# Reading the states' rows of two batches together, and dividing them by their softmax sums as they leave PSUM, in an attention and feed-forward kernel on one Trainium2 core

## The chip, the cores and the metric

The kernel runs on one core of one Trainium2 chip. The metric is the time of one execution in microseconds of the device. Most of the discussion uses one profiled execution, whose span runs from its first to its last instruction.

A core has five engines with a queue of instructions each: TensorE (PE; its weight loads are listed as PEld), VectorE (DVE), ScalarE (ACT), GpSimd (POOL) and SyncE (SP), which here only issues DMAs. Each works through its queue in order and waits for the others by semaphores. Products land in PSUM; all other operands lie in SBUF.

## The reference

Eight batches, eight heads, 512 tokens of 64 values, and 32 states of 64 values for each batch and head. Tokens read the states, states read the tokens, and all rows (544 for each batch) go through a two-layer feed-forward.

```python
scores = scale * np.matmul(x, state.transpose(0, 1, 3, 2))     # (8, 8, 512, 32)
scores = scores - scores.max(-1, keepdims=True)
a = np.exp(scores)
a /= a.sum(-1, keepdims=True) + 1e-09
xread = np.matmul(a, state)
scores2 = scale * np.matmul(state, x.transpose(0, 1, 3, 2))    # (8, 8, 32, 512)
scores2 = scores2 - scores2.max(-1, keepdims=True)
a2 = np.exp(scores2)
a2 /= a2.sum(-1, keepdims=True) + 1e-09
sread = np.matmul(a2, x)                                       # the states' rows
attn_out = np.concatenate([xread, sread], axis=2)
# rows of 8 heads x 64 values side by side: (4352, 512)
h = rows @ w_in                                                # 512 -> 2048
g = np.maximum(0.01 * h, h)
out = g @ w_out                                                # 2048 -> 512
```

The change concerns `a2` and `sread`.

## The kernel before

One batch at a time is in the main loop (line 932, batches 2 to 7; batches 0 and 1 are worked off by code written out ahead of it). A batch has 16 steps `s`. Step `s` makes one block of 128 hidden features for the batch's 512 tokens (`ff1`, line 369: two products into a PSUM tile with the tag "ph", and a leaky ReLU on ACT into `hT`). Between these, `fill(s)` inserts units of the second layer (line 557; of the batch before, then of this one), by the fixed table `PACE`. Also between the steps stands the attention of the next batch `nxt`: scores at s = 1, the tokens' softmax at s = 1 to 7, the states' softmax at s = 3 (maximum), 7 and 8 (`a_exp2`, ACT's exponential of 512 tokens with its sum beside it, in two halves `g`) and 11 (`a_probs2`). At s = 10 come the products of M (`a_m`, line 351, state times first-layer weights) for `nxt`: `pm0`, `pm1` and `pm2`, 8 products each; `pm2` has two tiles of the tag "ph" and is evicted by DVE and ACT (line 1031).

The order on every engine is the order of the program text. PSUM tags and their buffers set who waits for whom: the tag "ph" has two buffers of one bank, so each new "ph" tile waits for the eviction of the one before the last. The pool `att` has two buffers for each tag, unless stated.

The path of the states' rows:

- `a_exp2` (line 274) writes `e2`, 128 partitions (4 pairs of heads x 32 states) x 2 halves x 512 tokens, and its sums `r2`.
- `a_probs2` (line 279) adds 1e-9 to the sums, takes the reciprocal `qc`, and multiplies `e2` by it into `a2`, two instructions of 128x512 on DVE (line 285).
- `a_a2t` (line 290) issues a transposing DMA from SP, `a2` to `a2T`, at s = 0 of the batch's own loop (for batches 0 and 1 ahead of the loop).
- `a_sread_rows` (line 311) makes the rows on PE: 32 products of 128x64 for a batch, into a "ph" tile `psn` (line 318). ACT copies it to `sr_n` (line 326). It is called for batch 0 at s = 1 of batch 2, for batches 1 and 2 together at s = 10 of batch 2, and for batches 3, 4, 5 and 6 at s = 10 of their own loops, each time just ahead of `pm0`.
- `sread_t` (line 330) transposes `sr_n` into `sr_t` by DMA: batches 0 to 3 in batch 4, batches 4 to 6 in batch 7. Batch 7's own rows go another way (`a_sread`).

In the loop of batch 2, DVE also makes four sums of the second layer's weights (`weights_sum`, line 523): sums 0 and 2 at s = 3, sums 1 and 3 at s = 8. At s = 1, `a_sread_rows([a0])` is written ahead of `a_shift(nxt)` (lines 216 to 226, DVE). POOL casts the next loaded batch to bf16 (line 105) and the states (line 176).

Of the kernel before, what the change touches and what calls it, by code (L numbers as in the profile page):

```python
# [9 lines left out]
P = 128  # L10
B, H, S, D = 8, 8, 512, 64
# [8 lines left out]
BF16 = mybir.dt.bfloat16  # L20
FP32 = mybir.dt.float32
AF = mybir.ActivationFunctionType
ALU = mybir.AluOpType
# [4 lines left out]
def kernel(  # L28
# [9 lines left out]
    nc = tc.nc  # L38

    consts = ctx.enter_context(tc.tile_pool(name="consts", bufs=1))  # L40
    wpool = ctx.enter_context(tc.tile_pool(name="wpool", bufs=1))
    xpool = ctx.enter_context(tc.tile_pool(name="xpool", bufs=4))
    att = ctx.enter_context(tc.tile_pool(name="att", bufs=2))
# [53 lines left out]
    def load_x(b, eng):  # L97
        xl[b] = xpool.tile([P, H, NT * D], FP32, name="xl", tag="xl", bufs=1)
        eng.dma_start(xl[b][:], x[b].rearrange("h (p t) d -> p h (t d)", t=NT))

    def open_xb(b):
        xs[b] = xpool.tile([P, NT, H, D], BF16, name="xb", tag="xb")
# [37 lines left out]
    st_t = [consts.tile([P, hi - lo, P], BF16, name=f"st_t{lo}") for lo, hi in groups]  # L140
    sr_t = consts.tile([P, B, NK, NS], BF16, name="sr_t")
    sr_n = {}

    stb0 = consts.tile([P, 4, D], BF16, name="stb0")

# [132 lines left out]

    def a_probs2(a):
        nc.vector.tensor_scalar(out=a.r2[:], in0=a.r2[:], scalar1=1e-9, scalar2=None, op0=ALU.add)  # L280
        q2 = att.tile([P, 2], FP32, name="qc", tag="qc")
        nc.vector.reciprocal(q2[:], a.r2[:])
        a.a2 = att.tile([P, 2, S], BF16, name="a2", tag="a2")
        for g in range(2):
            nc.vector.tensor_scalar(
                out=a.a2[:, g, :], in0=a.e2[:, g, :],
                scalar1=q2[:, g:g + 1], scalar2=None, op0=ALU.mult,
            )

    def a_a2t(a):  # L290
        a.a2T = att.tile([P, 2, NT, P], BF16, name="a2T", tag="a2T")
        nc.sync.dma_start_transpose(
            a.a2T[:].rearrange("p g i q -> p (g i) q"), a.a2[:].rearrange("p g s -> p (g s)")
        )
# [16 lines left out]
    def a_sread_rows(some):  # L311

        ps = psum.tile([P, len(some), 2, D], FP32, name="psn", tag="ph")
        for u, a in enumerate(some):
            for g in range(2):
                for i in range(NT):
                    for k in range(NK):
                        nc.tensor.matmul(  # L318
                            ps[NS * k:NS * (k + 1), u, g, :],
                            lhsT=a.a2T[:, g, i, NS * k:NS * (k + 1)], rhs=a.xb[:, i, 2 * k + g, :],  # L320
                            start=(i == 0), stop=(i == NT - 1),
                        )
        c, b0 = divmod(some[0].b, 4)
        if c not in sr_n:
            sr_n[c] = consts.tile([P, 4, P], BF16, name=f"sr_n{c}", tag=("st0f", "stf2")[c])
        nc.scalar.copy(
            sr_n[c][:, b0:b0 + len(some)], ps[:].rearrange("p u g d -> p u (g d)")
        )

    def sread_t(c, n):  # L330
        nc.sync.dma_start_transpose(
            sr_t[:, 4 * c:4 * c + n].rearrange("p b k n -> p b (k n)"),
            sr_n[c][:, :n].rearrange("p b q -> p (b q)"),
        )

# [33 lines left out]
    def ff1(a, hT, j):  # L369
        ph = psum.tile([P, S], FP32, name="ph", tag="ph")  # L370
        for g in range(2):
            nc.tensor.matmul(  # L372
                ph[:], lhsT=a.M[:, g, P * j:P * (j + 1)],
                rhs=a.aT[:, g, :],
                start=(g == 0), stop=(g == 1),
            )
        nc.scalar.activation(out=hT[:, j, :], in_=ph[:], func=AF.Prelu, alpha=0.01)  # L377
# [265 lines left out]
    att_of = [Attn() for _ in range(B)]  # L643
    a0, a1, a2 = att_of[:3]
# [150 lines left out]
    def open_ff1_0(tag):  # L795
        if tag == "sc":
            pr = psum.tile([P, 2, S], FP32, name="php", tag=tag, bufs=1)
            return pr, [pr[:, 0], pr[:, 1]]
        ph = [psum.tile([P, S], FP32, name="ph", tag=tag) for _ in range(2)]
        return ph, [p[:] for p in ph]  # L800
# [15 lines left out]
    t0, b0 = open_ff1_0("py")  # L816
# [32 lines left out]
    for u in range(2):  # L849
        ps = psum.tile([P, NT, 2, P], BF16, name="pxt2", tag="ph")  # L850
# [81 lines left out]
    for b in range(2, B):  # L932
        hT = hpool.tile([P, 16, S], BF16, name="hT", tag="hT")
        a = att_of[b]
        nxt = att_of[b + 1] if b + 1 < B else None
        now = Batch(b, hT)
        std = []
        if b == 2:
            std = [(i, 3) for i in range(2)] + [(i, jq) for i in range(2, NT) for jq in range(4)]

        def fill(s):
            n = (PACE2 if b == 2 else PACE)[s]
            left = min(n, len(before.units)) if before else 0
            if left:
                before.run(left)
            if n > left:
                now.run(n - left)

        for s in range(16):
            if s == 11:  # L950
                fill(s)
            ff1(a, hT, s)
            if s == 0:
                if b + 2 < B:
                    load_x(b + 2, nc.sync)
                    open_xb(b + 2)
                a_a2t(a)
                if before:
                    for n in (0, 1):
                        before.f.sums(n, 4, 8)  # L960
            elif s == 1:
                if nxt is not None:
                    a_scores(nxt)
                m_evict(a, 3, a_m(a, 3, "big"), SCA)
                if b == 2:
                    a_sread_rows([a0])
                if nxt is not None:
                    a_shift(nxt)
                if b + 2 < B:
                    for h in range(0, H, 2):  # L970
                        cast_x(b + 2, h, h + 2, POO)
                if before:
                    before.f.sums(2, 4, 8)
            elif s == 3:
                if before:
                    before.f.sums(3)
                if nxt is not None:
                    a_max2(nxt)
                if b == 2:
                    weights_sum(0)  # L980
                    weights_sum(2)
            elif s == 4:
                if b == 2:
                    state_t(1)
                elif b == 4:
                    sread_t(0, 4)
                elif b == 7:
                    sread_t(1, 3)
            elif s == 8:
                if nxt is None:  # L990
                    a_sread(a)
                if b == 2:
                    weights_sum(1)
                    weights_sum(3)
            elif s == 12:
                for n in range(3):
                    now.f.sums(n, 0, 4)
            if nxt is None:
                if s == 4:
                    fi = FastIn(None)  # L1000
                    for n in range(3):
                        fi.w_sum(n)
                elif s == 10:
                    fi.w_sum(3)
                    fi.x_sums()
            if s == (9 if b == 2 else 7) and b + 2 < B:
                a_open(att_of[b + 2], b + 2)
                a_xt_dma(att_of[b + 2])
            if nxt is not None:
                if s == 5:  # L1010
                    a_exp(nxt)
                elif s in (7, 8):
                    a_exp2(nxt, s - 7)
                    if s == 7:
                        a_probs(nxt)
                elif s == 11:
                    a_probs2(nxt)
                elif s in (12, 13):
                    SCA(nxt.M[:, s - 12, DM:2 * DM], pm1[:, s - 12, :])
            if std:  # L1020
                i, jq = std.pop(0)
                piece(1, h1, i, jq)
            elif s != 11:
                fill(s)
            if s == 10 and nxt is not None:
                a_sread_rows([a1, a2] if b == 2 else [a])
                pm0 = a_m(nxt, 0, "big")
                pm1 = a_m(nxt, 1, "sc")
                pm2 = a_m(nxt, 2, "ph")
                for g, copy in enumerate((VEC, SCA)):  # L1030
                    copy(nxt.M[:, g, 2 * DM:3 * DM], pm2[g][:])
                m_evict(nxt, 0, pm0, SCA)
        before = now
# [24 lines left out]
    u, v = [psum.tile([P, 1, HC], FP32, name="yu", tag="ph")[:] for _ in range(2)]  # L1058
# [8 lines left out]
    for n in (1, 2, 6, 5, 7, 3, 4):  # L1067
# [7 lines left out]
        elif n == 7:  # L1075
            nc.gpsimd.tensor_tensor(
                out=ysb[1][:, :, HC:], in0=fs.sv[7][:], in1=fs.sv[5][:], op=ALU.add
# [8 lines left out]
    for i in range(2):  # L1086
        bank = before.bank[7] if i == 0 else psum.tile([P, 2, HC], FP32, name="yz", tag="big", bufs=1)[:]
        for m in range(NM):
            before.f.unit(bank, 4, m, first=True, of=i)
        nc.vector.tensor_tensor(  # L1090
            out=before.yo(1)[:, i, :HC], in0=bank[:, i, :], in1=before.f.sv[7][:, i, :], op=ALU.add
# [32 lines left out]
```

## Time and profile before

| | before |
|---|---|
| median of 3 runs | 204.49 us (204.19 to 204.7) |
| time of the profiled execution | 204.49 us |
| its span | 202.7 us |
| PE busy | 197.0 us, 97% |
| DVE busy | 151.4 us, 75% |
| ACT busy | 143.7 us, 71% |
| POOL busy | 39.7 us, 20% |
| 14 + 2 scalings of `e2` (line 285, DVE) | 4.9 us, 350 ns each |
| 6 copies of the rows (line 326, ACT) | 265 ns for 128x128 (five), 372 ns for 128x256 (one) |

The profile's page gives busy time by engine, the chain of work that ended last, and groups of instructions by line. The trace behind it can be asked for the order of instructions in a window (start, length, engine, line, output and inputs, count, and in brackets the idle time ahead and what ended it) and for who waited for whom. "ended last" matters most: an engine off that chain can be made faster without any effect.

### The profile page before, as it was taken

To read this page: it belongs to the slowest core of one execution; us is meant where nothing else is said; L and a number is where in the kernel's file an instruction comes from. 1 tells how busy PE (TensorE), PEld (TensorE's weight loads), DVE (VectorE), ACT (ScalarE), POOL (GpSimd) and SP (SyncE) were. 2 spreads that over 40 slices of the span, in tenths; PEclk is the share of its full clock that TensorE was granted. 3 is DMA by queue.
4 is the path that set the end of the run, shared out by engine and by line. 5 is a ranking of instruction groups with operands and counts; after the bars stand their busy time and mean duration, and the time that the engine had idled before them with its cause. 6 is when DMAs were issued, how large, how long until landed. Compare 5 with 4: busy or idle time off the path is not lost.

```text
span 202.7 us, 4755 instructions
## 1 busy us (share of the span) xinstructions
PE 197.0 (97%) x1964; PEld 126.0 (62%) x1964; DVE 151.4 (75%) x230; ACT 143.7 (71%) x265; POOL 39.7 (20%) x66
## 2 busy tenths in 40 slices
PE   7899999999999999999999999999999999999993
PEld 2543544444344567766776767766767677799882
DVE  1677679599799969976996699769968853686612
ACT  3458848589869796978697878788778856467710
POOL 8831002021005005200251040200020002004250
PEclk9999999999999999999999999999999999999999
DMA  6999996999477895537946795250017100410035
GB/s 189 223 207 277 229 298 113 141 303 245 53 175 214 114 275 109 103 125 253 118 29 181 240 127 105 103 159 5 0 57 198 27 0 32 178 55 0 3 89 170
DMA packets 39733, 27.99 MB, mean 138 GB/s; under 512 B 25312, under 2 KB 36704, under 8 KB 39712
## 3 DMA queue, kind: packets, MB, share of 16 engines
q1 hardware_dynamic: 34512, 20.88, 44.6%
q0 software_dynamic: 4912, 6.55, 15.8%
q10 hardware_dynamic: 288, 0.26, 0.6%
q8 instruction: 15, 0.25, 0.5%
q14 instruction: 6, 0.05, 0.1%
HBM read 17.30 MB, written 8.91 MB: 129 GB/s over the span
## 4 chain that ended last, share of the span: by engine, by line
PE 96%; DVE 1%; ACT 1%; issue 0%
PE yq L557 36%; PE ph L372 23%; PE py L487 10%; PE pm L351 4%; PE pyw L487 3%; PE pf L441 3%; PE yu L557 3%; PE pspin L132 3%; PE ph L804 2%; PE sc L206 1%; PE psn L318 1%; PE phw L383 1%; PE php L804 1%; DVE M L365 1%; ACT xT L666 1%; PE scn L695 0%
## 5 line engine op out<-in xcount | busy, mean ns | idle before, releaser
L377 ACT ACTIVATE hT<-ph 128x512 bf16<-128x512 f32 x108 | 63.5, 604 | 22.0 <-PE ph L372 21.4
L372 PE MATMUL ph<-aT,M 128*128 128x512 bf16 x216 | 62.3, 379 | 0.0
L557 PEld LDWEIGHTS <-su 128*128 128x128 bf16 x416 | 39.7, 98 | 14.5 <-DVE su L546 1.7
L557 PEld LDWEIGHTS <-hT 128*128 128x128 bf16 x288 | 27.7, 98 | 11.7 <-issue 1.1
L557 PE MATMUL yq<-tw_xf,su 128*128 128x256 bf16 x192 | 27.2, 273 | 0.0
L105 POOL CAST xb<-xl 128x512 bf16<-128x512 f32 (+1 forms) x21 | 14.4, 724 | 65.2 <-PE ph L372 40.6
L557 PE MATMUL yq<-w_out_bf,hT 128*128 128x256 bf16 x192 | 27.0, 273 | 0.0
L372 PEld LDWEIGHTS <-M 128*128 128x128 bf16 x216 | 21.0, 98 | 9.3 <-issue 0.8
L546 DVE TENSOR_TENSOR su<-hT 128x1024 bf16<-128x1024 bf16 x24 | 16.8, 700 | 10.5 <-ACT hT L377 10.5
L487 PE MATMUL py<-w_out_bf,hT 128*128 128x512 bf16 x96 | 24.2, 379 | 0.0
L487 PEld LDWEIGHTS <-hT 128*128 128x128 bf16 x128 | 12.1, 98 | 14.6 <-issue 0.9
L627 POOL TENSOR_TENSOR yo<-sv,sv 128x512 f32<-128x512 f32 x6 | 7.8, 1300 | 54.1 <-ACT sv L566 42.7
L569 DVE TENSOR_TENSOR yo<-yq,sv 128x512 f32<-128x512 f32 x17 | 11.6, 685 | 6.5 <-PE yq L557 6.5
L566 ACT COPY sv<-yq 128x512 f32<-128x512 f32 x24 | 13.9, 585 | 2.0 <-PE yq L557 1.4
L365 ACT CAST M<-pm 128x1024 bf16<-128x1024 f32 x13 | 13.2, 1014 | 0.9 <-PE pm L351 0.8
L557 PE MATMUL yq<-w_out_bf,su 128*128 128x256 bf16 x96 | 13.1, 273 | 0.0
L557 PE MATMUL yq<-tw_x,su 128*128 128x256 bf16 x96 | 13.1, 272 | 0.0
L557 PE MATMUL yq<-tw_x,hT 128*128 128x256 bf16 x88 | 12.1, 273 | 0.0
L274 ACT ACTIVATE e<-sc,mcols 128x512 bf16<-128x512 f32 x16 | 11.1, 696 | 0.0
L216 DVE TRANSPOSE_TENSOR_REDUCE mrow<-sc 128x32 f32<-128x1024 f32 x7 | 8.7, 1245 | 2.4 <-PE sc L206 2.4
L266 DVE TENSOR_REDUCE mcol<-sc 128x2 f32<-128x1024 f32 x8 | 9.7, 1215 | 0.0
L247 DVE STREAM_TRANSPOSE qb<-qh 128x1024 bf16<-128x1024 bf16 x7 | 8.7, 1245 | 0.2
(147 smaller groups left out, 271.3 us busy)
## 6 DMA issues: line engine op xcount, KB each, us to landing
xl<-in_x_dram SPq DMA_DIRECT2D x5, 1024.0 KB, 7.1
out_dram<-yo SPq DMA_DIRECT2D x10, 512.0 KB, 3.0
w_in_bf<-in_moe_w_in_dram POOLq DMA_DIRECT2D x4, 512.0 KB, 9.1
w_out_bf<-in_moe_w_out_dram POOLq DMA_DIRECT2D x4, 512.0 KB, 17.0
out_dram<-ysb SPq DMA_DIRECT2D x8, 256.0 KB, 5.1
xf<-in_x_dram SPq DMA_DIRECT2D x2, 512.0 KB, 4.8
x<-in_x_dram POOLq DMA_DIRECT2D x2, 512.0 KB, 13.8
xl<-in_x_dram POOLq DMA_DIRECT2D x1, 1024.0 KB, 19.8
```

What stands on the lines that cost most here:

```text
L105: copy(xs[b][:, :, h0:h1].rearrange("p t h d -> p h t d"), xl[b][:, h0:h1].rearrange("p h (t d) -> p h t d", t=NT),)
L216: nc.vector.tensor_reduce(out=m1[:], in_=flat.rearrange("p (c j) -> p c j", j=NS), axis=AX.X, op=ALU.max, apply_transpose=True,)
L266: nc.vector.tensor_reduce(out=m2[:], in_=a.sc[:], axis=AX.X, op=ALU.max, negate=True)
L274: nc.scalar.activation(out=a.e2[:, g], in_=a.sc[:, g, :], func=AF.Exp, bias=a.m2s[:, g:g + 1], scale=SCALE, accum_out=a.r2[:, g:g + 1],)
L365: copy(a.M[:, :, cols], pm[:])
L372: nc.tensor.matmul(ph[:], lhsT=a.M[:, g, P * j:P * (j + 1)], rhs=a.aT[:, g, :], start=(g == 0), stop=(g == 1),)
L377: nc.scalar.activation(out=hT[:, j, :], in_=ph[:], func=AF.Prelu, alpha=0.01)
L487: nc.tensor.matmul(y.py, lhsT=hT[:, j, P * i:P * (i + 1)], rhs=w_out_bf[:, j, :], start=(j == 0), stop=(j == 15),)
L546: (eng or nc.vector).tensor_tensor(out=S[n][:, ms], in0=u[:, ms], in1=v[:, ms], op=op)
L557: nc.tensor.matmul(bank[:, i, :], lhsT=lhs[:, m, P * i:P * (i + 1)], rhs=rhs[:, m, :], start=(first and m == 0 and (i == 0 or of is not No ...
L566: copy(t[:], bank)
L569: nc.vector.tensor_tensor(out=dst, in0=bank, in1=self.sv[n][:], op=ALU.add)
```

## The change

The scaling by the reciprocal sums is taken from `a2` ahead of the transpose to the rows behind the product: the transpose reads `e2` itself, the reciprocals of all batches stand in one tile `qall`, and DVE evicts `psn` with a multiplication by them where ACT copied it. Batch 7 keeps its scaled `a2`. Batches 3 and 4 are read together at s = 10 of batch 4, and batches 5 and 6 at s = 10 of batch 6. `sr_n` holds batches 0 to 2 and 3 to 6, and the two transposes of rows take three and four batches.

```diff
--- before.py
+++ after.py
@@ -140,6 +140,7 @@
     st_t = [consts.tile([P, hi - lo, P], BF16, name=f"st_t{lo}") for lo, hi in groups]
     sr_t = consts.tile([P, B, NK, NS], BF16, name="sr_t")
     sr_n = {}
+    qall = consts.tile([P, B, 2], FP32, name="qall")
 
     stb0 = consts.tile([P, 4, D], BF16, name="stb0")
 
@@ -278,14 +279,16 @@
 
     def a_probs2(a):
         nc.vector.tensor_scalar(out=a.r2[:], in0=a.r2[:], scalar1=1e-9, scalar2=None, op0=ALU.add)
-        q2 = att.tile([P, 2], FP32, name="qc", tag="qc")
-        nc.vector.reciprocal(q2[:], a.r2[:])
-        a.a2 = att.tile([P, 2, S], BF16, name="a2", tag="a2")
-        for g in range(2):
-            nc.vector.tensor_scalar(
-                out=a.a2[:, g, :], in0=a.e2[:, g, :],
-                scalar1=q2[:, g:g + 1], scalar2=None, op0=ALU.mult,
-            )
+        q2 = qall[:, a.b]
+        nc.vector.reciprocal(q2, a.r2[:])
+        a.a2 = a.e2
+        if a.b == B - 1:
+            a.a2 = att.tile([P, 2, S], BF16, name="a2", tag="a2", bufs=1)
+            for g in range(2):
+                nc.vector.tensor_scalar(
+                    out=a.a2[:, g, :], in0=a.e2[:, g, :],
+                    scalar1=q2[:, g:g + 1], scalar2=None, op0=ALU.mult,
+                )
 
     def a_a2t(a):
         a.a2T = att.tile([P, 2, NT, P], BF16, name="a2T", tag="a2T")
@@ -320,16 +323,18 @@
                             lhsT=a.a2T[:, g, i, NS * k:NS * (k + 1)], rhs=a.xb[:, i, 2 * k + g, :],
                             start=(i == 0), stop=(i == NT - 1),
                         )
-        c, b0 = divmod(some[0].b, 4)
+        c, b0 = (0, some[0].b) if some[0].b < 3 else (1, some[0].b - 3)
         if c not in sr_n:
             sr_n[c] = consts.tile([P, 4, P], BF16, name=f"sr_n{c}", tag=("st0f", "stf2")[c])
-        nc.scalar.copy(
-            sr_n[c][:, b0:b0 + len(some)], ps[:].rearrange("p u g d -> p u (g d)")
+        u0, n = some[0].b, len(some)
+        nc.vector.tensor_tensor(
+            out=sr_n[c][:, b0:b0 + n].rearrange("p u (g d) -> p u g d", g=2), in0=ps[:],
+            in1=qall[:, u0:u0 + n, :, None].to_broadcast([P, n, 2, D]), op=ALU.mult,
         )
 
     def sread_t(c, n):
         nc.sync.dma_start_transpose(
-            sr_t[:, 4 * c:4 * c + n].rearrange("p b k n -> p b (k n)"),
+            sr_t[:, 3 * c:3 * c + n].rearrange("p b k n -> p b (k n)"),
             sr_n[c][:, :n].rearrange("p b q -> p (b q)"),
         )
 
@@ -983,9 +988,9 @@
                 if b == 2:
                     state_t(1)
                 elif b == 4:
-                    sread_t(0, 4)
+                    sread_t(0, 3)
                 elif b == 7:
-                    sread_t(1, 3)
+                    sread_t(1, 4)
             elif s == 8:
                 if nxt is None:
                     a_sread(a)
@@ -1023,7 +1028,8 @@
             elif s != 11:
                 fill(s)
             if s == 10 and nxt is not None:
-                a_sread_rows([a1, a2] if b == 2 else [a])
+                if b % 2 == 0:
+                    a_sread_rows([att_of[b - 1], a])
                 pm0 = a_m(nxt, 0, "big")
                 pm1 = a_m(nxt, 1, "sc")
                 pm2 = a_m(nxt, 2, "ph")
```

## The prediction

> **What bounds the kernel now.** I read the page's head, the chain of waits, TensorE's list of waits, and then the timeline around every place where the states' rows are made.
>
> ```profile
> PE 197.0 (97%) x1964; PEld 126.0 (62%) x1964; DVE 151.4 (75%) x230; ACT 143.7 (71%) x265; POOL 39.7 (20%) x66
> ...
> PE 96%; DVE 1%; ACT 1%; issue 0%
> ```
>
> The chain that ends last runs through TensorE (PE) for 96% of the span, and PE's list of waits holds five waits, all in the first 14 us (one more, marked only as issue, is shown below). From 36.8 us to the end, work taken off VectorE (DVE), ScalarE (ACT) or a queue is worth nothing in itself. The time moves only where PE's own work changes or PE is made to wait. The two places that matter, in the chain, for batches 2 (two batches read together) and 3 (one batch):
>
> ```profile
> 67.01 0.63 PE psn L318 x64
> 67.64 0.92 PE pm L351 x24
> ```
>
> ```profile
> 87.61 0.35 PE psn L318 x32
> 87.95 0.80 PE pm L351 x24
> ```
>
> 64 products of rows take 0.63, 32 take 0.35. The 24 products of M behind them take 0.92 behind the pair and 0.80 behind the single: behind the pair PE loses 0.12. The code says why. psn and both banks of pm2 (line 1029) share the tag "ph" with two buffers, so the second bank of pm2 is psn's and waits for its eviction. The timeline of batch 2 shows that wait as a gap in the weight loads, which ends as ACT's eviction ends (67.73 + 0.37 = 68.10):
>
> ```profile
> 67.57 0.33 PEld L351 LDWEIGHTS <-st_t 64*32 64x32 bf16 x18
> 67.73 0.37 ACT L326 CAST sr_n<-psn 128x256 bf16<-128x256 f32 x1 [0.64 <-PE psn L318]
> 68.15 0.11 PEld L351 LDWEIGHTS <-st_t 64*32 64x32 bf16 x6 [0.26 <-issue]
> ```
>
> So the question is when DVE, which gets this eviction, is free. DVE's timeline in batch 2:
>
> ```profile
> 53.25 0.62 DVE L285 TENSOR_SCALAR a<-e,qc 128x512 bf16<-128x512 bf16 x2
> 54.10 1.25 DVE L216 TRANSPOSE_TENSOR_REDUCE mrow<-sc 128x32 f32<-128x1024 f32 x1 [0.24 <-PE sc L206]
> ...
> 64.92 1.03 DVE L248 TENSOR_TENSOR aT<-e,qb 128x1024 bf16<-128x1024 bf16 x1
> 65.88 1.21 DVE L523 TENSOR_TENSOR tw_xf<-w_out_bf,tw_x 128x2048 bf16<-128x2048 bf16 x1
> 67.13 1.23 DVE L523 TENSOR_TENSOR tw_x<-tw_xf,w_out_bf 128x2048 bf16<-128x2048 bf16 x1
> 68.61 0.69 DVE L1031 CAST M<-pm 128x512 bf16<-128x512 f32 x1 [0.26 <-PE pm L351]
> ```
>
> From 54.10 to 68.36 DVE is busy 13.97 of 14.26 us, with no wait marked: 14 instructions back to back, and the last ends 0.72 after the pair's products (66.94 + 0.70 = 67.64). ACT could evict at once; DVE can't.
>
> **The change, part by part.**
>
> *The scaling of a2 taken away.* 14 of 16 instructions of line 285 go, 14 x 0.35 = 4.9 us of DVE at most (a pair spans 0.62). PE waits for none of it. In batch 2 it ends at 53.87, before line 216's data (PE's scores end at 54.03), so DVE's full stretch doesn't begin earlier either. Worth 0.
>
> *Six copies off ACT.* 5 x 0.27 + 0.37 = 1.7 us; but for the pair's own eviction (below), PE waits for no ACT instruction that they delay. Worth 0.
>
> *Rows of batches 3 and 5 moved to 4 and 6.* PE loses two singles, 2 x 0.35, and gains two second halves, 2 x (0.63 - 0.35) = 0.56: -0.14. That M's products cost the same straight behind yq as behind psn isn't in the trace in this form; 16 of them behind 128-row products took 0.56 (0.035 each), 24 behind psn 0.80 (0.033), so I take no difference. A gap of 0.21 in weight loads ahead of each psn could go twice (-0.42) at best; 0.1 for each M could come (+0.2) at worst.
>
> *Evictions on DVE in batches 4 and 6.* DVE is free there: its sum of line 569 ends at 108.41, its next work starts at 109.86. The nearest row to the new instruction is a sum of 128x256 from PSUM with an SBUF operand (line 1090), 0.425, against ACT's 0.372. DVE and ACT begin alike behind PE (M's two evictions start at 88.81 and 88.84). A pair thus costs PE 0.12 + 0.05 = 0.17, where a single cost nothing: +0.34 for two.
>
> *Evictions on DVE in batch 2.* First the rows of batch 0: their copy stands ahead of line 216 in DVE's order now. PE ends them at 54.18 + 0.42 = 54.60; the copy starts 0.08 later (as in batch 3) at 54.68 and takes about 0.295 (0.425 less half of the 0.26 between 128x512 at 0.685 and 128x256). Line 216, which could start at 54.10, starts at about 54.89 (an elementwise instruction's successor starts some 0.09 before its end). All 14 instructions move by 0.79. ACT's exponential at 60.41 and its exponentials at 63.00 and 64.30 still find their operands, so nothing absorbs or adds. Then the pair's copy, queued behind the weight sums: it starts at 68.28 + 0.79 = 69.07 and ends at 69.50, where ACT ended at 68.10. PE stands at pm2 that much longer: +1.40. Behind the waiting copy are queued pm2's own eviction and batch 3's reciprocals; PE's next FF1 (69.28) needs the former, which keeps its distance to PE.
>
> *Queues.* SP's transpose of batch 1 waited for the scaling until 53.89; SP is free from 51.46 and issues then. Load of batch 4 (56.52), transpose of batch 2 (57.20), the state's and xT's transposes come up to 2.4 earlier. With them POOL's casts of batch 4 (62.57 to 64.86) and of the states (64.80 to 65.41) move to about 60.1 to 63. They leave lines 242 (0.43 there, 0.18 elsewhere) and 248 (1.03 there, 0.69 at 86.31): -0.59 for DVE. They meet the first two weight sums instead. The nearest rows are line 546's sums beside POOL's casts at 79.33 (1.03 against 0.69 alone), at 100.38 (0.68) and 80.28 (1.62 against 1.22): 0 to +0.4 each, +0.57 for two in the middle. Taken as 0, with ends -0.59 and +0.55.
> The Trainium skill (SBUF — State Buffer, Who interferes with whom) says that a VectorE instruction with two SBUF inputs and a GpSimd one that reads SBUF share a read port, and the later one blocks whole. By that each weight sum waits at most one cast (estimate 0.57, from 2.29/4); these rows fit. By the same page the new copy, with its other input in PSUM, is not slowed.
>
> *Transposes read e2 itself.* ACT's exponentials of batch 2 (46.46) overwrite batch 0's e2 and now wait for its transpose, issued at 39.08 + 7.4 to landing = 46.48. SP could issue 0.28 earlier, but the transpose's packets run behind the load and stores of 37.10 to 38.74. I take 0.05 lost (ends 0 and 1.1, the latter if it lands after the trace's longest, 8.8). ACT's delay there is PE's: FF1 at 49.38 follows ACT's 49.25. Later batches have over 2 us between landing and overwriting. The transpose of four batches' rows instead of three is in batch 7, 14 us ahead of its readers: 0.
>
> Sum: -0.14 + 0.34 + 1.40 + 0 + 0.05 = +1.65 us. The profiled execution has a span of 202.7 and a time of 204.49, which is also the median of the runs; 204.49 + 1.65 = 206.1.
>
> **Rivals.**
> 1. *DVE in batch 2 holds PE* (forecast): 206.1; by the ends of its terms 205.2 to 207.0.
> 2. *Not slower: DVE meets the pair in time.* The point that decides: DVE's last weight sum would have to end by 67.73, not 69.15. POOL's casts moving away give 0.59 of the 1.42, so a second relief would be needed. Then only +0.05 - 0.14 + 0.34 is left, or, if pairs on an idle DVE cost PE nothing, -0.14: 204.3 to 204.7. For it: DVE sheds 4.9 us. Against: none of that lies between 54.10 and the pair.
> 3. *The casts meet the weight sums in full*: +0.55 on the forecast, 206.7. The port rule quoted above is this rival's rule. For it: the casts land there by my times. Against: one of three such rows shows no cost.
> 4. *ACT waits for the transpose of batch 0*: +1.1 on the forecast, 207.2. For it: no slack at 46.46. Against: that transpose took 7.4 in this very place.
>
> **How the numbers follow.** Forecast 0.70, rival 2 0.11, rival 3 0.11, rival 4 0.08. What a measurement of this kernel can tell from no change is about 0.3%, 0.6 us. Rivals 1, 3 and 4 are slower by more, but for the forecast's lowest edge (0.01); rival 2 is the same, or, with PE's gaps of 0.42 gone too, barely faster (0.02). So faster 0.02, same 0.10, slower 0.88. The range goes from 205.0 (the forecast's terms low together) to 207.3 (rival 4) and leaves rival 2 and some tails outside.
>
> **What the profile would show.** Right: DVE's copy of batch 0's rows ahead of line 216, line 216 near 54.9; the pair's copy behind the last weight sum near 69.1; M's products of batch 2 about 2.3 long in the chain instead of 0.92; in batches 4 and 6 about 0.97 behind psn x64, none behind batches 3 and 5. Wrong: weight sums ending by 68 us, a PE wait in another batch, or ACT idle at 46.5.

## The result and the profile after

The changed kernel takes 206.44 us (median of 6 runs, 206.16 to 207.18) against 204.57 for the kernel before beside it (6 runs): ratio 1.0093, 95% interval 1.0065 to 1.012. It is 1.9 us slower; 206.1 was forecast. The profiled execution has a span of 204.8 us and a time of 206.59.

The head of the page and the chain that ended last, of the changed kernel:

```profile
PE 195.2 (95%) x1939; PEld 125.3 (61%) x1964; DVE 149.4 (73%) x220; ACT 142.3 (69%) x259; POOL 39.7 (19%) x66
...
PE 83%; DVE 11%; DMA 2%; issue 2%; ACT 1%; DVEq 0%
```

DVE is 2.0 us less busy and ACT 1.4, as the edit intends, and yet DVE has gone from 1% to 11% of the chain that ends last. PE's list of waits has a line that it didn't have:

```profile
PE pm L356 <- DVE sr_n L330: 1.2, 1, 1.2
```

The chain in order of time, changed kernel (start, length, what; line numbers are 5 higher than before in this part, M's products are line 356, psn's are 321, the second layer's products yq 562, the new eviction is 330):

```profile
54.69 0.41 PE psn L321 x32
55.11 0.29 DVE sr_n L330
...
68.41 1.23 DVE tw_x L528
69.64 0.35 DVE sr_n L330
70.02 0.41 PE pm L356 x7
...
89.48 0.77 PE pm L356 x24
...
110.15 0.63 PE psn L321 x64
110.78 1.03 PE pm L356 x24
```

For 15 us the chain leaves PE: it runs from batch 0's rows into DVE's new copy, through the 14 instructions of batch 3's attention and the weight sums that stand in batch 2's loop, into the pair's copy, and only then back to PE's product. These are DVE's instructions at both ends of that stretch, from its timeline:

```profile
55.11 0.29 DVE L330 TENSOR_TENSOR sr_n<-psn,qall 128x128 bf16<-128x128 f32 x1 [1.46 <-PE psn L321]
55.32 1.24 DVE L217 TRANSPOSE_TENSOR_REDUCE mrow<-sc 128x32 f32<-128x1024 f32 x1
...
61.58 1.63 DVE L528 TENSOR_TENSOR tw_x<-w_out_bf 128x2048 bf16<-128x2048 bf16 x1
...
66.55 0.69 DVE L249 TENSOR_TENSOR aT<-e,qb 128x1024 bf16<-128x1024 bf16 x1
...
69.56 0.42 DVE L330 TENSOR_TENSOR sr_n<-psn,qall 128x256 bf16<-128x256 f32 x1
```

DVE idles 1.46 us ahead of the first copy: the scaling that was taken away had freed time where nothing could use it.

Where the time went, from the same events in both chains (start of M's products, or their end, by batch):

| point | before | after | distance | added |
|---|---|---|---|---|
| FF1 after the start-up | 36.80 | 37.13 | 0.33 | 0.33 |
| M's products ahead of batch 2 | 51.30 | 51.74 | 0.44 | 0.11 |
| end of M's products, batch 2 | 68.56 | 70.43 | 1.87 | 1.43 |
| batch 3 | 88.75 | 90.25 | 1.50 | -0.37 |
| batch 4 | 109.81 | 111.81 | 2.00 | 0.50 |
| batch 5 | 130.86 | 132.49 | 1.63 | -0.37 |
| batch 6 | 151.91 | 153.99 | 2.08 | 0.45 |
| span | 202.7 | 204.8 | 2.1 | 0 |

The first row isn't the change's: the kernels below run the code of the changed one or of the one before up to there, and their products at the second row start anywhere from 51.15 to 51.67. The kernel with late weight sums has the changed kernel's code up to there and reaches the first row at 36.65. From the first row on the change adds 2.08 - 0.33 = 1.75; the sum in the prediction was 1.65.

### The profile page after: what moved, and what is told of

It is laid out like the page before. It is cut to its first block, busy times and chain, and to the rows that moved or that the text cites. A ratio compares the mean times of both kernels' runs of the same rounds, so it can differ in the third digit from the quotient of the medians.

```text
span 204.8 us, 4706 instructions
## 1 busy us (share of the span) xinstructions
PE 195.2 (95%) x1939; PEld 125.3 (61%) x1964; DVE 149.4 (73%) x220; ACT 142.3 (69%) x259; POOL 39.7 (19%) x66
## 4 chain that ended last, share of the span: by engine, by line
PE 83%; DVE 11%; DMA 2%; issue 2%; ACT 1%; DVEq 0%
PE yq L562 35%; PE ph L377 19%; PE py L492 6%; PE pm L356 4%; PE pyw L492 3%; PE pf L446 3%; PE yu L562 3%; DMA xf<-in_x_dram 2%; PE ph L809 2%; DVE tw_x L528 1%; PE sc L207 1%; DVE tw_xf L528 1%; PE php L809 1%; PE phw L388 1%; PE psn L321 1%
## 5 line engine op out<-in xcount | busy, mean ns | idle before, releaser
L377 PE MATMUL ph<-aT,M 128*128 128x512 bf16 x199 | 59.7, 379 | 0.3
L356 PE MATMUL pm<-w_in_bf,st_t 64*32 64x512 bf16 x192 | 8.5, 380 | 1.2 <-DVE sr_n L330 1.2
```

What stands on the lines that cost most here:

```text
L356: nc.tensor.matmul(at[v][NS * r:NS * (r + 1)], lhsT=st_of(a, g, k), rhs=w_in_bf[D * g:D * (g + 1), k, DM * c:DM * (c + 1)], start=True, st ...
L377: nc.tensor.matmul(ph[:], lhsT=a.M[:, g, P * j:P * (j + 1)], rhs=a.aT[:, g, :], start=(g == 0), stop=(g == 1),)
```

## The experiments

The theory: PE stands in batch 2 because the eviction of a pair waits in DVE's queue behind work that was put there for other reasons. Rival A: the multiplication out of PSUM is itself slow. Rival B: reading in pairs is what costs.

**Weight sums behind the copy.** The changed kernel, with one edit:

```diff
             elif s == 8:
...
-                if b == 2:
-                    weights_sum(1)
-                    weights_sum(3)
             elif s == 12:
                 for n in range(3):
                     now.f.sums(n, 0, 4)
+                if b == 2:
+                    weights_sum(1)
+                    weights_sum(3)
```

> The changed kernel with weight sums 1 and 3 moved from s = 8 to s = 12 of batch 2, behind the pair's copy. Theory (PE stands in batch 2 because the pair's copy is queued on VectorE behind the weight sums): the copy starts 0.1 after the pair's products, PE loses 0.17 to 0.25 there instead of 1.7, the time falls by 1.4 to 1.5 from the changed kernel, to about 205.0. Rival A (the multiplication out of PSUM is itself slow to start or to release PE): batch 2 keeps its 1.2 to 1.7 of waiting, 206.4. Rival B (reading in pairs is the cost, wherever evicted): 206.4 too.

Measured: 204.77 us, ratio to the kernel before 1.0018 (1.0000 to 1.0036): 1.7 below the changed kernel. The chain stays on PE through batch 2:

```profile
66.86 0.63 PE psn L321 x64
67.49 0.97 PE pm L356 x24
```

The copy starts at 67.58, 0.09 after its products end in the chain, and M's products take 0.97 where the changed kernel needed 2.4 (68.01 to 70.43). The two sums cost nothing four steps later. Rivals A and B are out as the main cause: with the same copy of the same pair, and nothing ahead of it, M's products take 0.97, against 0.77 with no rows ahead of them.

**Batch 0's rows on ACT.** The other half of the queue's delay:

```diff
-        if a.b == B - 1:
+        if a.b in (0, B - 1):
             a.a2 = att.tile([P, 2, S], BF16, name="a2", tag="a2", bufs=1)
...
+        if u0 == 0:
+            nc.scalar.copy(sr_n[c][:, :1], ps[:].rearrange("p u g d -> p u (g d)"))
+            return
```

> The changed kernel, but batch 0 keeps its scaled a2 and its rows are copied by ScalarE as before; all else as changed. Theory: VectorE's 14 instructions of batch 2 start 0.8 earlier, PE's wait at the pair shrinks by 0.8, and ScalarE's exponentials of batch 2 no longer wait for batch 0's transpose (0.1): 205.5. The wait left at the pair is about 0.9, from the two weight sums alone. Rival A: no change at the pair, 206.3. Rival B: 206.3.

Measured: 205.28 us, ratio 1.0041 (1.0025 to 1.0057). PE's list of waits, this kernel:

```profile
PE pm L359 <- DVE sr_n L333: 0.6, 1, 0.6
```

1.2 has become 0.6: DVE's stretch starts 0.85 earlier (54.47 against 55.32) and its last weight sum ends 0.69 earlier (68.95 against 69.64); of both, 0.07 is start-up (0.37 here, 0.44 in the changed kernel). M's products of batch 2 end 69.75 - 68.56 - 0.37 = 0.82 late instead of 1.43, 0.6 less where 0.8 was expected; DVE's line 269 takes 0.45 here where it takes 0.17 in the changed kernel, beside GpSimd's casts. This trace explains 0.6, while the medians lie 1.2 apart (206.44 and 205.28): the profiled execution took 205.89, more than the median of its kernel. Both halves of the queue are thus shown, the copy ahead of the stretch and the sums ahead of the pair's copy.

**Singles.** The changed kernel, with batches 3 to 6 read one by one:

```diff
-                if b % 2 == 0:
-                    a_sread_rows([att_of[b - 1], a])
+                a_sread_rows([a1, a2] if b == 2 else [a])
```

> The changed kernel, but batches 3 to 6 are read one by one as before, each evicted by VectorE's multiplication. Theory: behind each of the four singles the products of M take 0.80 as before, none of them waits; against the changed kernel batches 3 and 5 give back 0.38 each and batches 4 and 6 save 0.45 to 0.5 each: -0.2, about 206.2. Batch 2 still loses 1.4. Rival B (pairs are the cost): most of the loss goes, 204.8 or less.

Measured: 206.12 us, ratio 1.0072 (1.005 to 1.0095). The loss of batch 2 stays (M's products end 70.05 - 68.56 - 0.22 of start-up = 1.27 late), so the pairs of batches 3 to 6 aren't it. M's products behind the singles, from the chain:

```profile
89.44 0.89 PE pm L356 x24
...
110.58 0.83 PE pm L356 x24
```

They take 0.83 to 0.89, where 0.80 was expected: a single's copy on DVE ends a little later too, 0.37 to 0.43 behind its rows where ACT's ends 0.35 behind them.

**Pairs alone.** The kernel before, with the pairing and the new grouping of `sr_n`, scaling and ACT's copies left as they were:

```diff
-                a_sread_rows([a1, a2] if b == 2 else [a])
+                if b % 2 == 0:
+                    a_sread_rows([att_of[b - 1], a])
```

> The kernel before, with only the pairing of batches 3 to 6: softmax divided ahead of the transpose as before, ScalarE copies all rows. Theory: the second halves cost 0.28 each, each pair makes PE wait 0.12 as in batch 2 before, and two singles of 0.35 to 0.38 go: +0.05 to +0.1, 204.6, no measurable change. Rival B: 1.5 or more slower, 206.

Measured: 204.71 us, ratio 1.0007 (0.9992 to 1.0021), no change. In batches 3 and 4, from its chain:

```profile
87.78 0.77 PE pm L351 x24
...
108.46 0.63 PE psn L318 x64
109.09 0.92 PE pm L351 x24
```

Batch 3 saves 0.35 + 0.80 - 0.77 = 0.38 and batch 4 pays 0.28 + 0.12: the pairing gives and takes the same. In batch 2 of this kernel, though, ACT's copy starts 0.21 behind the rows (67.70) instead of 0.09, and M's products take more than behind DVE's copies:

```profile
67.70 1.04 PE pm L351 x24
```

```profile
67.91 0.37 ACT L326 CAST sr_n<-psn 128x256 bf16<-128x256 f32 x1 [0.76 <-PE psn L318]
```

So it is not the engine that sets M's time but the end of the copy. Wherever the rows stand straight ahead of all 24 products of M, in all the kernels here, M's products end 0.44 to 0.47 after the copy ends: 68.74 after 68.28 here, 68.56 after 68.10 in batch 2 of the kernel before, 111.81 after 111.35 in batch 4 of the changed one, and 109.81 after 109.35 behind a single on ACT. Why ACT's copy started late here isn't shown.

**psn in another buffer.** On top of the late weight sums, the pair's tile takes the buffer of `pm0`, which is made last:

```diff
-                    a_sread_rows([att_of[b - 1], a])
-                pm0 = a_m(nxt, 0, "big")
+                    a_sread_rows([att_of[b - 1], a], "big", 1)
                 pm1 = a_m(nxt, 1, "sc")
                 pm2 = a_m(nxt, 2, "ph")
+                pm0 = a_m(nxt, 0, "big")
```

> The kernel of e1 (weight sums 1 and 3 behind the pair's copy), and the pairs' psn takes the two-bank buffer of pm0 (tag big) instead of a ph buffer; the products of M come in the order pm1, pm2, pm0, so that the tile that waits for psn's eviction is the last of the three. Theory: psn's copy ends 0.5 to 0.6 after its products, pm1 and pm2 take 0.55; the products of M take 0.77 to 0.85 in batches 2, 4 and 6 instead of 0.97 to 1.03, -0.5 to -0.6 against e1: 204.2, at or just below the kernel before. Rival B (a pair costs PE in itself): 0.97 to 1.03 stays, 204.8.

Measured: 204.68 us, ratio 1.0007 (0.999 to 1.0025); the theory's 0.5 didn't come. M's products still take 0.56 + 0.41, end to end 0.98. Weight loads and DVE around the pair of batch 2:

```profile
67.84 0.32 PEld L356 LDWEIGHTS <-st_t 64*32 64x32 bf16 x17
...
68.00 0.42 DVE L330 TENSOR_TENSOR sr_n<-psn,qall 128x256 bf16<-128x256 f32 x1 [0.70 <-PE psn L321]
68.48 0.11 PEld L356 LDWEIGHTS <-st_t 64*32 64x32 bf16 x7 [0.32 <-issue]
```

The copy ends at 68.42, just as the first 16 products end (67.91 + 0.56 = 68.47). PE's row shows no wait worth naming, and yet the last 8 products take 0.41 where in an unbroken 24 they take 0.77 - 0.56 = 0.21: the weight loads stood still for 0.32, until the copy had ended. M's products end 0.47 after the copy (68.89), as in the other order. Left to be tested is what a pair costs when its copy ends earlier.

**Rows ahead of the second-layer units.** On top of the late weight sums, the pair's rows are made before the second-layer units of step 10 (8 products, in batch 2 only 6) instead of behind them:

```diff
+            if s == 10 and nxt is not None and b % 2 == 0:
+                a_sread_rows([att_of[b - 1], a])
             if std:
...
             elif s != 11:
                 fill(s)
             if s == 10 and nxt is not None:
-                if b % 2 == 0:
-                    a_sread_rows([att_of[b - 1], a])
```

> The kernel of e1 with the pairs' rows ahead of the second-layer units of step 10 instead of behind them, so that VectorE's copy of the pair ends some 0.4 before the first product of pm2 needs its buffer. Theory (a late eviction costs PE about 0.2 by emptying its pipeline at pm2, however short the wait): M's products take 0.77 in batches 2, 4 and 6 instead of 0.97 to 1.03; the units behind the rows take 0.11 more for the change of tile shape; 0.1 to 0.15 saved for each pair, 204.4. Rival B (a pair costs PE that much in itself): M's products stay at 0.97 or more, 204.8 or above.

Measured: 204.58 us, ratio 0.9999 (0.9987 to 1.0012), level with the kernel before. The chain around the pairs of batches 2 and 4:

```profile
66.51 0.63 PE psn L321 x64
67.15 0.76 PE yq L562 x6
67.91 0.77 PE pm L356 x24
...
107.54 0.63 PE psn L321 x64
108.17 0.98 PE yq L562 x8
109.15 0.77 PE pm L356 x24
```

The copy in batch 2 now ends at 67.35 + 0.43 = 67.78, ahead of M's first product, and in batch 4 at 108.74. M's products take 0.77, as without any rows ahead of them. So it is the eviction's lateness that costs 0.2, not the pair. The eight products of the second layer behind the rows take 0.98 instead of 0.87. The Trainium skill (TensorEngine Tiling (Array Packing), Key Properties) says that a change of tiling mode drains TensorE, without a number; the 0.11 fits that, here between 128x32 and 128x128 tiles.

**Load of batch 4 later.** The changed kernel, to see what the moved casts do:

```diff
                 if b + 2 < B:
-                    load_x(b + 2, nc.sync)
+                    if b > 2:
+                        load_x(b + 2, nc.sync)
...
             elif s == 1:
...
+                if b == 2:
+                    load_x(b + 2, nc.sync)
```

> The changed kernel with the load of batch 4 issued behind the transpose of batch 2's probabilities, at about the time that it has in the kernel before, so that GpSimd's casts of batch 4 come at about 62.5 again. Theory: the second weight sum falls from 1.63 to 1.22, the multiplication into aT (0.69 in the changed kernel) rises to about 1.0; both cancel within 0.2 and the pair's copy still starts near 69.5: 206.4. Rival 3 of the prediction (the casts on the weight sums carry a good part of the loss): the copy starts 0.4 or more earlier, 206.0 or less.

Measured: 206.36 us in one run, so without an interval. DVE's timeline:

```profile
61.46 1.22 DVE L528 TENSOR_TENSOR tw_x<-w_out_bf 128x2048 bf16<-128x2048 bf16 x1
...
65.96 1.03 DVE L249 TENSOR_TENSOR aT<-e,qb 128x1024 bf16<-128x1024 bf16 x1
...
69.31 0.42 DVE L330 TENSOR_TENSOR sr_n<-psn,qall 128x256 bf16<-128x256 f32 x1
```

The weight sum falls by 0.41 and the multiplication into aT rises by 0.34, as expected; the pair's copy starts at 69.31 instead of 69.56, of which 0.12 is start-up. In this trace the casts' new place isn't where the time went.

## Why the prediction was right, point by point

- *The chain on PE, everything else worth nothing.* Right: DVE lost 2.0 us and ACT 1.4 of busy time, and no part of that came back. The scaling was worth less than the 4.9 counted: all 16 instructions of line 285 keep DVE busy for 4.9, and the two that are left take 0.6, so 4.3 went, and the copies brought 1.6.
- *Batch 2, +1.40.* Measured 1.43. The steps hold too: line 216 (217 now) was forecast at 54.89 and starts at 55.32 less 0.44 of distance, 54.88; the last weight sum was forecast to end at 69.15 and ends at 69.64 - 0.44 = 69.20.
- *Batches 3 and 5, -0.35 each.* Measured -0.37: M's products behind yq take 0.77, 0.03 less than behind psn, not the same as I took. "Where a single cost nothing" was wrong by that 0.03: behind a single, too, M's products end 0.45 after ACT's copy.
- *Batches 4 and 6, 0.28 + 0.17 each.* Measured 0.50 and 0.45. My reason, a wait for the eviction, holds: M's products end 0.44 to 0.47 after it, whichever engine makes it. In batch 6 DVE's copy ends 0.51 behind the rows, and M's products take the 0.97 that was forecast. In batch 4 the copy starts 0.15 behind the rows instead of 0.09 (110.93 and 110.78), and they take 1.03; why it starts later isn't shown. The third expectation took a single on DVE to cost nothing more than on ACT; it costs 0.03 to 0.09 more.
- *Casts moved, 0 with ends -0.59 and +0.55.* Measured 1.63 - 1.22 - 0.34 = +0.07. That the 0 came out is partly luck: it was the middle between two ends, and two of its parts missed in opposite directions. Of the two weight sums one was slowed, as in the rows quoted. Line 243 (242 before) stayed at 0.44, which I had counted as relieved (with singles, the same code up to there, it takes 0.19); and the casts themselves took 4.17 instead of 2.29, which I had not counted, at no cost. By the Trainium skill's port rule (SBUF — State Buffer, Who interferes with whom) the later of two such instructions blocks whole; here both sides lost, 0.41 and 1.88, over a run of several instructions on each.
- *ACT's exponential behind batch 0's transpose, 0.05.* It lost 0.11: the transpose landed at 39.54 + 7.3 = 46.84 and the exponential started at 46.90, when ACT's instruction before it had ended at 46.91, where it starts 0.11 before that end in the kernel before. The last four FF1 products of that stretch, which PE makes behind it, take 1.00 instead of 0.89. In the kernels with late weight sums, with singles and with early rows they take 0.89 to 0.90, and with the late load 1.08, so this wait comes and goes. Rival 4's full 1.1 was never seen.
- *Rival 2, DVE in time.* The kernel with late weight sums is that case: it gives 204.77, where the rival said 204.3 to 204.7.

## What to carry to other kernels

When an eviction is moved to another engine, read that engine's queue from the moment the data are ready, not its share of busy time: 4.3 us of scaling were taken off VectorE here, none of it in the 14 us that decided. A small instruction placed ahead of a full stretch delays everything queued behind it, and the delay appears where another engine waits for the end of that stretch. What is in the way can often be moved (two weight sums, four steps later, gave back 1.7 us); what was saved in the end, nothing in any kernel here, fits that TensorE sets the time: the pairing alone saved it 0.38 in one batch and cost it 0.40 in the next, and the late division took no work from it.

## What the runs showed of the hardware

- 24 products of 64x32 tiles take 0.77 us in one go. Where one of their last buffers is still being copied out, they end 0.44 to 0.47 after that copy, whichever engine copies: 0.92 when the copy ends 0.46 behind the products ahead of them, 0.97 at 0.51, 1.04 at 0.58. TensorE's timeline can show next to no wait there; the wait stands as a gap in the weight loads (0.32 in the kernel with psn in another buffer).
- Eight 128x256 products of the second layer take 0.87, and 0.98 behind products of another tile shape.
- VectorE's multiplication of 128x256 out of PSUM with the second operand repeated along the free axis takes 0.42, as a plain sum of that size does (0.425).
